# A gated linear recurrence and a PReLU feed-forward layer on one core: the written-out order of all steps is replaced by another order

## The chip, the cores and the metric

The kernel runs on one core of a Trainium2 chip. The metric is the device time of one execution in microseconds. An engine is named here as the profile names it: PE is TensorE (PEld its weight loads), DVE is VectorE, ACT is ScalarE, POOL is GpSimd, SP is SyncE, which in this kernel issues every transfer (731 of them).

## The reference, cut to what matters

```python
# attention block: batch 4, 8 heads, 768 tokens, head size 48
mag = np.sqrt(a_re * a_re + a_im * a_im)
scale = np.minimum(mag, 0.999) / (mag + 1e-06)
a_re_n, a_im_n = (a_re * scale, a_im * scale)      # one complex gate per token and channel
for t in range(S):
    new_re = ar * S_re - ai * S_im                 # ar, ai: the gates of token t
    new_im = ar * S_im + ai * S_re
    S_re, S_im = (new_re + k_t v_t^T, new_im)      # a 48x48 state per head
    y[:, :, t] = q_t @ S_re
# feed-forward block on x = y as 3072 tokens x 384
h = x @ w_in                                       # 384 -> 2048
g = np.maximum(h, 0.0) + alpha * np.minimum(h, 0.0)
out = g @ w_out                                    # 2048 -> 384
```

q, k, v and the gates are 32-bit floats; w_in and w_out arrive as 64-bit floats, and the kernel makes 32-bit ones of them. All products on PE are 32-bit.

## The kernel before, in words

The work is cut into 41 tasks. Each is a Python generator that emits one or a few instructions between two of its yields; such a piece is a *step*. There are 4292 steps. A task's own steps always come in the same sequence; how the steps of different tasks are mixed is written out by hand as a string of 4292 letters, `ORDER`, one letter for one step of the task with that letter:

```python
def run(self, order):
    for c in order:
        next(self.tasks[self.LETTERS.index(c)], None)
...
with tc.manual_schedule():
    ...
    plan.run(ORDER)
```

Every engine takes its instructions strictly in the sequence in which the steps emitted them, and so does SP with the transfers. A semaphore wait therefore holds up everything that stands behind it on its engine. `ORDER` thus sets the order on PE, DVE, ACT, POOL and SP together, and nothing else does. (The `yield DVE(...)`, `yield PE(...)` and so on only mark where a step ends; their numbers are not used.)

The tasks and their letters:

- **A to I: `gates`.** The gates of batch 0 in three pieces of 1, 2 and 3 chunks (A, B, C), then two pieces of 3 chunks for each other batch (D to I). A chunk is 128 tokens. A piece normalises the gates (ACT and DVE, lines 253 to 301), multiplies the magnitudes up into decays over 2, 4, 8, ... tokens (L318, stored as `decs`, L323), and multiplies the phases up along time: 7 products within blocks of 8 tokens, 7 over blocks of blocks (both `product`, L338 and L340, a multiplication and an addition), and a chain along the rest, `run` (the same two lines). After each of the two last stages `three` copies the result on ACT (L366, L368). Then come the normalisation of the offsets (L405 to L413), the last products (L426, L429, DVE), and the store of the phases, `phs` (L421, L431). In A, B and C the small products are DVE's, in D to I POOL's.
- **J: `loads`.** For each chunk: q and k into `KQ` (3 buffers, L579, L581), the phases into `PP` (1 buffer, L587), the decays into `T` (2 buffers, L594). `PP` reads what the gate piece stored in `phs`, `T` what it stored in `decs`.
- **K, L: `half_rows`, `loads_v`.** v in several arrangements, by way of a scratch in device memory (L560, L603 to L629).
- **M, N, O: `pieces`, `weights`.** The 16 pieces of the 64-bit weights (L491), and their conversion on ACT (L507, L509, L511), POOL (L515) and DVE (L517, L519).
- **P to Z and a to m: `unit`.** One for each of 24 chunks (4 batches of 6). A unit rotates q and k by the phases (L661, L663 on DVE, which read `PP`), and then goes through levels h = 1, 2, 4, 8, 16, 32: DVE scales `KQ` in place by the decays in `T` (L717), ACT makes copies (L740, L756), PE multiplies keys and queries (L678, `ps_lv`), ACT or DVE masks the result (L699, L702). Then PE transposes the keys (L785), ACT copies them over `T` (L787, L788), PE makes the chunk's state (L797, `ps_kv`) and the outputs (L817, L841, `ps_y`), DVE carries the state on (L826, L829), and ACT copies the output (L855), which SP stores (L860, `ysc`).
- **n: `loads_x`.** Reloads the outputs as `xT` (L873) in 14 token groups: 1, 1, ten times 2, 1, 1 chunks.
- **o: `all_mlp`.** The feed-forward layer. For each token group 16 features of 128 (three products each, L889, `ps_h`, 2 buffers), their PReLU (ACT L896, then DVE L898 into `g_sb`), and the output products (L908, `ps_o`), ACT copy (L918) and store (L921).

So the gates feed the units (by device memory), the units feed each other within a batch (the state) and the feed-forward layer (by device memory), and the feed-forward layer takes most of PE's time. Between two feed-forward products on PE stand the units' products, and all wait in one queue.

## Time and profile before

| | us |
|---|---|
| three runs | 851.10, 855.48, 854.49 |
| their median | 854.49 |
| the profiled execution | 854.34 |
| its span, first to last instruction | 852.6 |
| busy in the span: PE / PEld / DVE / ACT / POOL | 697.3 / 529.4 / 653.5 / 439.1 / 209.2 |

The profiled execution lies 0.15 us from the median, and 1.7 us of it lie outside the span. "Busy" counts the time in which at least one of the engine's instructions runs; an engine that only waits or issues is not busy. Each 32-bit product gives two records, so the 672 feature products are 1344 records in the profile.

The page's second part cuts the span into 40 slices of 21.3 us; a digit is the share of the slice in tenths. In the chain of waits, the profile follows the work that ended last back to what released it.

### The profile page before, as it was taken

What the parts mean: (1) busy time and instruction counts of PE and PEld (TensorE: products, weight loads), DVE (VectorE), ACT (ScalarE), POOL (GpSimd) and SP (SyncE); (2) the same over time, 40 slices, a digit from 0 to 9 for tenths busy, and PEclk for the clock granted to TensorE, in tenths of its full rate; (3) what the DMA queues carried; (4) which work ended last, traced back from release to release, by engine and by line L of the source; (5) the groups of instructions that cost most, each with busy time, mean ns of one, the idle gap of its engine ahead of it and who ended that gap; (6) DMA issues with size and microseconds to landing.
All of it is one profiled execution on the core that took longest, in us unless ns stands there. A gap on an engine that the chain in (4) does not pass through costs nothing.

```text
span 852.6 us, 26860 instructions
## 1 busy us (share of the span) xinstructions
PE 697.3 (82%) x11488; PEld 529.4 (62%) x11488; DVE 653.5 (77%) x1020; ACT 439.1 (52%) x937; POOL 209.2 (25%) x293
## 2 busy tenths in 40 slices
PE   0001314776998899889999999999999999999998
PEld 0001313565776677667777777777777777777776
DVE  5999999997996899599989997887776846633212
ACT  6767758766355754474576436554344334322221
POOL 6131232376403710260056144000052000000000
PEclk9999656798998999999999999999999999999999
DMA  8687876755768365756765766667454555412010
GB/s 238 155 272 188 263 200 189 216 128 138 203 174 199 102 182 163 209 133 156 231 156 145 212 162 177 157 182 185 113 130 104 148 143 117 102 46 65 11 39 9
DMA packets 194174, 130.91 MB, mean 154 GB/s; under 512 B 74120, under 2 KB 185864, under 8 KB 194056
## 3 DMA queue, kind: packets, MB, share of 16 engines
q1 hardware_dynamic: 194056, 129.20, 57.1%
q8 instruction: 90, 1.47, 0.7%
q14 instruction: 28, 0.23, 0.1%
HBM read 100.82 MB, written 35.71 MB: 160 GB/s over the span
## 4 chain that ended last, share of the span: by engine, by line
PE 63%; DVE 18%; POOL 6%; ACT 5%; DMA 4%; issue 3%; SPq 0%; DVEq 0%; ACTq 0%; POOLq 0%
PE ps_o L908 26%; PE ps_h L889 24%; PE ps_lv L678 4%; POOL gate L338 3%; PE ps_y L817 3%; DVE KQ L717 3%; PE ps_kv L797 2%; PE ps_y L841 2%; DVE gate L338 2%; DVE gate L426 2%; DMA T<-decs 2%; POOL run L340 2%; DVE gate L340 1%; PE ps_kt L785 1%; POOL gate L340 1%
## 5 line engine op out<-in xcount | busy, mean ns | idle before, releaser
L908 PE MATMUL ps_o<-w_out_sb,g_sb 128*128 128x384 f32 x768 | 297.9, 500 | 11.7 <-DVE g_sb L898 9.0
L889 PE MATMUL ps_h<-xT,w_in_sb 128*128 128x256 f32 (+1 forms) x1344 | 301.2, 357 | 0.0
L889 PEld LDWEIGHTS ps_h<-xT,w_in_sb 128*128 128x128 f32 x1344 | 235.1, 193 | 72.2 <-issue 3.3
L898 DVE SCALAR_TENSOR_TENSOR g_sb<-g_sb,al,ps_h 128x256 f32<-128x256 f32 (+1 forms) x224 | 97.3, 436 | 133.4 <-ACT g_sb L896 132.7
L896 ACT ACTIVATE g_sb<-ps_h 128x256 f32<-128x256 f32 (+1 forms) x224 | 79.1, 354 | 203.7 <-PE ps_h L889 202.7
L908 PEld LDWEIGHTS ps_o<-w_out_sb,g_sb 128*128 128x128 f32 x768 | 137.9, 192 | 63.0 <-DVE g_sb L898 12.0
L717 DVE TENSOR_TENSOR KQ<-KQ,T 96x1024 f32<-96x1024 f32 x120 | 146.6, 1225 | 33.9 <-PE ps_lv L678 22.9
L678 PE MATMUL ps_lv<-WQ 96*32 96x32 f32 x2304 | 34.3, 202 | 80.4 <-DVE WQ L661 51.8
L678 PEld LDWEIGHTS ps_lv<-WQ 96*32 96x32 f32 x2304 | 26.5, 115 | 98.1 <-DVE WQ L661 51.8
L338 POOL TENSOR_TENSOR gate<-gate 128x72 f32<-128x72 f32 x42 | 26.3, 626 | 148.3 <-ACT gate L368 145.5
L740 ACT COPY WQ<-KQ 96x1024 f32<-96x1024 f32 x48 | 50.0, 1041 | 15.4 <-DVE KQ L717 15.1
L515 POOL TENSOR_SCALAR top<-top 128x768 f32<-128x768 f32 x16 | 39.3, 2461 | 70.0 <-ACT top L507 59.7
L338 DVE TENSOR_TENSOR gate<-gate 128x576 f32<-128x576 f32 (+5 forms) x84 | 50.5, 601 | 1.7
L756 ACT COPY W<-KQ 96x512 f32<-96x512 f32 x48 | 30.8, 642 | 40.6 <-DVE KQ L717 33.1
L855 ACT COPY T<-ps_y 48x256 f32<-48x256 f32 x96 | 30.7, 366 | 36.8 <-PE ps_y L841 36.2
L817 PE MATMUL ps_y<-A,VL 64*48 64x64 f32 x2304 | 42.3, 227 | 3.7 <-issue 3.7
L785 PE MATMUL ps_kt<-ident,KQ 96*128 96x96 f32 x192 | 26.4, 264 | 22.2 <-DVE KQ L717 12.2
L426 DVE TENSOR_TENSOR gate<-gate 128x1152 f32<-128x1152 f32 (+2 forms) x36 | 44.2, 1250 | 0.1
L699 ACT ACTIVATE A<-ps_lv,columns 128x64 f32<-128x64 f32 x144 | 37.4, 337 | 13.0 <-PE ps_lv L678 12.9
L817 PEld LDWEIGHTS ps_y<-A,VL 64*48 64x48 f32 x2304 | 40.6, 128 | 4.4 <-issue 4.4
L785 PEld LDWEIGHTS ps_kt<-ident,KQ 96*128 96x128 f32 x192 | 22.1, 150 | 31.1 <-ACT T L788 10.9
L678 PE MATMUL ps_lv<-KQ,W 96*32 96x32 f32 x1536 | 24.2, 204 | 17.9 <-ACT W L756 17.9
(106 smaller groups left out, 926.9 us busy)
## 6 DMA issues: line engine op xcount, KB each, us to landing
T<-decs SPq DMA_DIRECT2D x48, 384.0 KB
PP<-phs SPq DMA_DIRECT2D x24, 387.0 KB
KQ<-in_q_dram SPq DMA_DIRECT2D x48, 192.0 KB
decs<-gate SPq DMA_DIRECT2D x7, 1152.0 KB
phs<-gate SPq DMA_DIRECT2D x14, 576.0 KB
KQ<-in_k_dram SPq DMA_DIRECT2D x40, 192.0 KB
vsc<-in_v_dram SPq DMA_DIRECT2D x48, 144.0 KB
VL<-vsc SPq DMA_DIRECT2D x24, 288.0 KB
```

Source lines behind the costliest of these rows:

```text
L338: on(4 * k).tensor_tensor(out=m, in0=w[:, 1::-1].unsqueeze(2).to_broadcast([P, 2, 2, k]), in1=pairs_of(u), op=ALU.mult)
L426: TT(out=m[:, a], in0=U5[:, 1 + a], in1=turned(off3, o)[:, a].unsqueeze(1).unsqueeze(3).to_broadcast([P, L // 2, nb, 2]), op=ALU.mult)
L515: nc.gpsimd.tensor_scalar(out=top, in0=top, scalar1=F64_SMALL, scalar2=None, op0=ALU.max)
L678: nc.tensor.matmul(t[64 * i + j:64 * i + j + HC // 2, p], lhsT=keys(n, g), rhs=queries(n, g), start=True, stop=True)
L717: nc.vector.tensor_tensor(out=x, in0=x if x0 is None else x0, in1=m, op=ALU.mult)
L740: nc.scalar.copy(z.rearrange("p i n t -> p i (n t)").rearrange("p i (m h) -> p m i h", h=h), bass.AP(tensor=KQ.tensor, offset=KQ.offset + ...
L785: nc.tensor.transpose(t[:, p], KQ[:, 1, 4 * i + p], ident[:D2, :D2])
L817: nc.tensor.matmul(o, lhsT=Vp[h][64 * i:64 * i + 64, s, e_ * D:(e_ + 1) * D], rhs=a, start=False, stop=False)
L889: nc.tensor.matmul(p, lhsT=w_in_sb[:, f // 2, kk, f % 2 * P:(f % 2 + 1) * P], rhs=x_of[m][:, kk], start=(kk == 0), stop=(kk == NK - 1))
L896: nc.scalar.activation(gt, p, AF.Relu, scale=-1.0)
L898: nc.vector.scalar_tensor_tensor(out=gt, in0=gt, scalar=al_1[:, f:f + 1], in1=p, op0=ALU.mult, op1=ALU.add)
L908: nc.tensor.matmul(sums[0], lhsT=gt[:, c * P:(c + 1) * P], rhs=w_out_sb[:, f], start=(f == 0), stop=(f == NF - 1))
```

## The change

The string `ORDER` is replaced by another string. It has the same 4292 letters, each as often as before. No other line differs, so that the instructions, their sizes and their data stay the same: 5888 matmuls, 707 two-input DVE operations, 935 ACT operations, 731 transfers in both programs. What differs is their sequence on PE, DVE, ACT, POOL and SP.

```diff
 ORDER = (
-    "AAAAAAAAAAAAAAAAAAAAABAAAAJMJJMABBBMMBANJMMAOAAAAAAAAAAAAAAAAAALLLNBLAAAAAAAAAAALNAAAAAAAKKKKKKKLLLA"
-    "OALLAMNNAAAAAAOAAAAAAAAABLBNAAAAAAALAANBBNOOBNBBBLBMBBBJOJNOBBBBBNBBJNNNBBNBBBBOBBBBBBBBBBBBBBBNOPBP"
-    "OBPPPPCCCBOKBBBBBBBBBBBBBPPOBBPKBCBBBMPCBPKKBCBJKKOPOPBBBBBBOMBKPNPMBBKNJBCKBBBBPPMBKKNKKBBNBPBBBBPP"
...
-    "oooooooooooooooooooooooooooooooooooooooooooooooooooooooooooooooooooooooooooooooooooooooooooo")
+    "AAAAAAAAAAAAAAAABJJJJBBAAAAAAAAMMMMMAMAAAAAAAAAAALLLBBNNBBLABLAAALABALAAAANBNABBBBANAABABBANABOOAMBB"
+    "OBBOAAAAAAKMAABBBABABABABABBAKKKKAALLKAABABABAABAABNAAAAABANBABALAAAABAABNBNOBBBBOOOOBONBMNBNNBBBBNNJ"
+    "OBOOOOOBBPBPCBNPCBBBBPCBBBBCCJJJOBBOBBKPPPPBCBBBBBMPNJJLNNBPNNBPBPBPBCNPBNCMBMCPPPPPJPCKKKKKKKKKKKKK"
...
+    "oooooooooooooooooooooooooooooooooooooooooooooooooooooooooooooooooooooooooooooooooooooooooooo")
```

More of the change, by code (lines that the diff above doesn't have):

```diff
@@ L30 @@
 ORDER = (
-    "AAAAAAAAAAAAAAAAAAAAABAAAAJMJJMABBBMMBANJMMAOAAAAAAAAAAAAAAAAAALLLNBLAAAAAAAAAAALNAAAAAAAKKKKKKKLLLA"
-    "OALLAMNNAAAAAAOAAAAAAAAABLBNAAAAAAALAANBBNOOBNBBBLBMBBBJOJNOBBBBBNBBJNNNBBNBBBBOBBBBBBBBBBBBBBBNOPBP"
-    "OBPPPPCCCBOKBBBBBBBBBBBBBPPOBBPKBCBBBMPCBPKKBCBJKKOPOPBBBBBBOMBKPNPMBBKNJBCKBBBBPPMBKKNKKBBNBPBBBBPP"
-    "BCCBPPOPCCCPPPNNPPCCCCPPCPPPPJLPPPPPJNCJPCNNNCCNCNCCQJQJPQJDDJJCPCJMNCNCPCPCPPCOCQQPDQDDJPPPPOCOOOCK"
-    "QCQCCCCCCQQCCCCCMOQCOJCJRCCRCOQOCOQQCQCOOOCCCCCCNNKKMMCCOCQCRCQCQCNNNKCLLLLLLQLCCCCCRQOCnCDCCCOCOCCC"
@@ L36 @@
-    "CQRMLLNDCJQCNRNRLLCQCCLLLRMCQCQDQRJJOCOCKQODCCCCRDNQQQQCCQQQQQQJODMQLNNDQODDODoQEKoooooooDOoRooNDJoo"
-    "oooooDRRQQRQLLoooDNoooLoRLLLLLDRLOQNQooQoQLooRRoRoDDoQDQDOOLDoooDDoRDELDLRRRRORRRRRJDooDDDDDDDRoooRN"
-    "NooDDRooooooEoRDRRRRRDNDoDoESDSDRDJOSREKOoooooLnoLLKoRSoooRRRRSSOLLKLSSSooESRLooooooLRoSOLLoLJELLSoo"
-    "NJSSSSoEoEESSDooDDooDDDDDDooooDDDDDDDKJREEoooDDDDooEDDDSDDoEooEoooSSSRSSSoLSooooJJSETSJSJJooKJSoEooo"
-    "DDDDDDooDESDSoooSSSDDDSSJEEoEETSSSSDESSSoSSSTEoooooooJJoKoEooDSDTooooEoSoTUKTLoTTTLoooooooooLTLoLoDK"
@@ L41 @@
-    "UooooooLDDTDJJooooJJnKDDDoEEooooDooTTETooDooooooLUoooooooooEoTToooUUDDLoooooooDTooToooooooDLDUUUoooo"
-    "ooUTUUooooooUoTTTTEoUUTTTTEooTTUToLLLLoooEEEToLooTTTTTTJJTTUoUUoTTUJoEooTETTTTTKEUUUUUFooooEUoooLLVo"
-    "oEoUooLLLELULLUVUoTUTVooUEEoooEULLLLLoooUUUJJJFEEUUUUUJJVVVUVVooooVVVJoUUUUUVVooFVooooUooVVoVFFVVoFV"
-    "LLVooEEEEEEEEEEEEEEEEoooEEEEoooooFFJoWVLLVWJFVoooJooooVooVVVVVWVoLVFooWoFoEEEoEVoVLWWLLLLLLELLVWVnVo"
-    "oJJEEEEEEJJFWooFEEEEEoWWoFFVFVJVFWVVoFoVooooooEWEWFVLVLVWWVWVVVVoooLKLooLLLoLLLJFFWWoXoWLJoEEoEEELEo"
@@ L46 @@
-    "ooooEooJooWWoEWEWWWEoooWEoEoooWWooFoWoWFoooooEXWWoooooLXoFoooooFFXoLXXWWWWXXWXFEXWXWWWXJJoooooJXXJXF"
-    "WXXFFFFoWWWWWoXoXooLoooWooooooXWLXXXXXooFoooXXFYoLLFFFFFFFoXXooXoXXoooLLLLLLLoooLLLYXXXJJXFJXFFFFFFF"
-    "FFFFooXYGooXXXGooYoooXXnFYJXXYYoFooYYXXXXYGooooYJJJoooooooooooJJYFFFFooJoooJooYYYYLGGoGZYYoooooooGGo"
-    "FFFFFFFooooFoYZoooFooFFoZooooZYYZYYZGYYZZoYYYoGZoYFFoYoooKKLLoYLLLLZLoLLLJLFFFFFLFLFFoZGGYoooooGZooG"
-    "GoGGYYoYYJJYoKKYGooYFFoFKKYoYLYLYLFLLLLYYLLLLFGaGZoYZFYYYFZZLZGKooooZooooLLoZKooFFFFFoooooZZZZaZZZZZ"
@@ L51 @@
-    "ooooZZoooooZooZoooJJFFGnooJoZZZZZFFFLooLFFZLZoZJLLLoGoaaGooooooooaZZaaGGJoGoooaooaLHaHaooGGoooGGGooa"
-    "ooooooooZZaZGGZZZoZaaaaaGGoooaHJoGoooooooaaaoaGGaaGaaaoooooGGaoLoaLoJoooooHHGboGGGGGGGaoHoaooLLobooL"
-    "LoooooJHHabJabHaaaaaabaJbJJaJaJaHaaabbbbbbbbHKoooooooHoooooooJGGGGoGGbbbHbGGooocGGGGbJHoooooooooooJG"
-    "GGKoooHbbccoooooooooobbccbGGGHcGbobbbGcGoooGGGGGGGGGHccooobbHGbGKLooooHHboobLLJLLLLLoLLLLLbLKnoobbcc"
-    "cHbbHJbcbcGHHHbHHbbcJoHHLLLLLLooLoLJLLHHHcooooocccHHoooooooooHGGGGbbbbbbbboGccccccGGocGGooocLoooooGo"
@@ L56 @@
-    "cLoccooooocLLGoGHGGooocJoooocGcccccccccccccJcccooKdooHooHoooJJJoHHHoJooHHHodHHHHoooooooooooHHHHdHHHH"
-    "HooHHdoodddJdJddddJJooeooooooooooooddoodddoooeoooddHHoooooooooHddeeeeoHHHHHLHHHHHHHLLLdddLLLLLdLLLLo"
-    "JLooeeddddodooHHddoJJeoooHdddHdddddneoooHHoIddeeeeeoodeJfLfIHdHHdHeddddooooeHooooLLLLooooooJJoooIIoo"
-    "oeooooIoooHoHHHooeeIoeeeHHHLfILoooHIooLooeIofHeJJoeooeooooIfffefoooeeLofoLoLoeLLLeeeeeeeeoJHfKHJJooo"
-    "oooofeoILLfooIeeHffffKLLLfoeLooeeeeeooooooofoooooooofoooLoofKffgooooffffffIffLILLLLJooIgHooooLfLfooo"
@@ L61 @@
-    "IooIKKIIIIoffffIfJnJfJHgfgJofIJJooooooofoooooogIfggfgoLoooffIIfLfffIogoKoggooooooooooooohhoogooooggg"
-    "ggoIhJhggoooooLoJoooooooooohhLJJooooghggggggghohogIILIIoogIoooggIogLLLLooooooIohhhhhooooLLLLgIoKKggg"
-    "ggggggJJJhhooohogggLIoooooooooIIIIIIKKoooogoghoIoooooioooLooooiJJIIoooooonIIIoohhhoiioooIIIIIoIhhhII"
-    "hhhLLLLLLLhhhiJiooILLLLLooIhJooohiohhooIIooooiiJhhhhhhIhIIiohooooiooLoLiLLLILiJIhhIhhhhhJiiIiiiiooII"
-    "IIIIIIIoooooooooooLiiiiIoIooooohhiiiiiiooojiooIIIIoooooIIoLjJJjjLooooLIooLiLoLLIjjjooooIooijjjjIIooo"
@@ L66 @@
-    "ooooiiiIiIIiiooiLooioooLLLiLLILoLLLIIjoiiijjoiiiioooIiojoooooooooojjjoooooooonojjjoooojjLjjjjjoooooI"
-    "jLjLLooooooojjoojjjjjjoooJJJJJoooJJoojJJjoooookokkJJoooooooooooojkjkLLjjjkjjojjkkoJkkoJJJkoookooooLL"
-    "LooooooooJlJlkkooooooooookokklooklokooooooloolkkkkokkklllLooookookLkoloLJkoooooooooLLkLLkLoLoooollkk"
-    "kkkkkkkkkkkkkoooooooooollllllooJoooooookkolooooollollmmnJJloooooooomooollooooooooollmllooooommlloooo"
-    "ooooooLLoLLoLoooLLLLLoLLLLooooomooooooommmmmoooollllllooolloooooolllllllllmmoooooooooLooLLLoooommooo"
@@ L71 @@
-    "oooooooooooooLoooooomoooooomooooLLLLLLLLmooonooooooooooommommooooooooooooooooooooooooommmmmmoooooooo"
-    "ooooooooommmooooooooooooooommmmmmmmmmmmomoommnoooooooooooooooooooooooooooooooooooooooooooooooooooooo"
+    "AAAAAAAAAAAAAAAABJJJJBBAAAAAAAAMMMMMAMAAAAAAAAAAALLLBBNNBBLABLAAALABALAAAANBNABBBBANAABABBANABOOAMBB"
+    "OBBOAAAAAAKMAABBBABABABABABBAKKKKAALLKAABABABAABAABNAAAAABANBABALAAABAABNBNOBBBBOOOOBONBMNBNNBBBBNNJ"
+    "OBOOOOOBBPBPCBNPCBBBBPCBBBBCCJJJOBBOBBKPPPPBCBBBBBMPNJJLNNBPNNBPBPBPBCNPBNCMBMCPPPPPJPCKKKKKKKKKKKKK"
@@ new lines @@
+    "BKBKPBBBMBCPBNOCNBOOBPCMNCLLCCBLPPPPPPPPPPPPPPPPCCMCBCCBKCCCPJOCOCDOJOCNNJCNNNNNCDCCKKKPCPCPPPPPPPPP"
+    "CCQCOKOOOCMQCCQLDDDQCCLLLLLLJLLLLLLCLCCCJDJJJJJJJCCNJQQCDNCQCQCDDQQCDCCNNQCDDQQDDQCOCODDCDCDCCCQDDOQ"
+    "CQOCQQQCDDDDKOCRQQCRQQQQQQCQQQRRRRQQQQQMnQCNDMCOCOOCDDDMCQCLQCLRCCCCRCRRLLLRCRRRoKJLQOOOOCoRoCoCRRCR"
+    "oQQLLLLLoooKLLQLoQQQoQCoCDCooRooQoRRDooCCCCRRRRRRRRRRoCRCoCoCoCDoRQCJJJEooRRODooooNNNNNoEDRooRoRoooo"
+    "RDnLLLLooOoOoOoRODLooRoLLLLLLRLLDNRNoLSoooooooooSoRRRRRooJJSooOoooooSoSSDSNDSSSESoooooooRoSNSSoooSDo"
@@ new lines @@
+    "ooSSSDJSJJEJJJJJJDoooooDoooEOSSSSooooSDoooSSSSSSooDDDDDDDooETTSSSEESooooSSSSSToSSEEESSooKSSSoSToJTTT"
+    "ToooToooSToooTooSLoooToULoDLLoLDTJDDDDDDJTDoToEDTDDoDLDLoDDDDDDooLLLLLoToTLTooooooooooToTTTUTTToTooT"
+    "ooTLJooDTTToooDUUTTTTTToULLLLULEEEEooEoTEoEDDDDDDDDDoDDEooooooUEToooUUUoooooonoUoEooJoUoooooUEUEDTDD"
+    "DoTTUUUELEJULoooLLKLLLLKoUoooooDDooDDDJoKDKKoKoooUUUUUUooooDDDTTTTTToUoooUDUUUooooUooDUEDUUUUEUEEEoo"
+    "EoEoooooooEoEEUooUooJooEoooUUUUoUUoFUUoooEEEoEoEooooooooooEEoEoEVFooFoJVVooJoFoJJnooooJJJJVJVFoLLooo"
@@ new lines @@
+    "oooooVVVFFLoLVoooooooooEEEEEEVoooVVVEEEEEEEEEEELEEEoEJJJooFoWWoEEoEEEVooooVVooVoooWJVVVVFLoooWooLooo"
+    "oWVVVVVVWVWWJVoooVFFVooooXVWLoLLLVLLoLooKVKoEEEEWEVVVVVVVVVVVKLLWEEVoKooLLLLLooLXFWLVLLVLVLVVWWWWWoE"
+    "EEEELooWooooEoEoEWEEEooJEWWWWWWWWEoooooooooJJEoEJEEEoooEWWWooooWoooWWWWWWWWWXLoooooWoFFFLXoLLXXXoXXo"
+    "GLLWWooJoJLLXooXoXWWWWWWooooFoFFXXXXXXFoLooooLooFoXoFoFFFFFFFJJooFooonXoXXXXXGLLLLooFFXooooooXXXXooo"
+    "XoXoFYFFFooooFoooFooXoFXXXXXXXXXFFXXXXXJJoYYJoooooLJLJFFFGoooFYLGFFFFFFFFooXoooYYYYYJYoYooXoooooooLo"
@@ new lines @@
+    "FFFFFoZZYYYYJooJYoYYZooooooYoooooZGoYYYYYYYYoYFLZZZZZZZFooooLoYYLFFLGFLLLLFLLooooYYoZZoYYYJYYYYJJLJJ"
+    "LLGoFZZZLLFLLFLLLLFLooooLFFFFFFFFFFFooZZYooFFFFYZoGGGGFoooFYYYYYYYYZZZoooFooLooooFFFFFFZJFFFZooZZZZZ"
+    "FZFoooooJZooZoZZnZZZZooZZZZZJZaZZLLFFJoLooooZZZJoooFoGaooGooaoaooooGGGLLLLLLLoLLLaaaaoooooooooaJaJaJ"
+    "ooooooaGaaaaaoooHoooHoaaooooooGGoooaaGaaaGGaaaGGGooGGGooboaaaKboooooJooooooaooooaHGbGaGJGbJoaaGaabbb"
+    "bJoJaaaaaabaaGLLbLLLoGoLGoLLLGaaHooHJooobboGoooooobboooGHobbbHobbooooJbooGHoJoboLHGJoooGbbbGbGbbbbJb"
@@ new lines @@
+    "ooocooooGoooJoonbooKoKGccoKKKKKooooooLbcccGcccooooHoooocooGoLLLbGJoJobbbobHbHGHHbbbLbHbGbbbbbLbbboGG"
+    "GGGHoHoHoLoooGGGGGoGcGLcoGoGooGGGoGoGoGcGcGcccccLJoJoLooLoooLooooLLLcccLLccLdocoJocGcoGcGccGoocodooc"
+    "oHHHddcHcccccccHdLcGGcGKoooLLHHGGHLoHLJLLHHoHooHooHooHdcGcdcdddcHcccooodoooGoooGGGGoGLLdLLLLLoGGGodd"
+    "dddoooododoooonooooGooGodGddddooGdoddoooooooGHGddHoodJodHHHoJoJJJHHHJJJooooodooooooddddddddddddddddo"
+    "HJeeooooJooooeoooooeoHooHHHHHHHdoLeeeooooooeeeeoefoofoooeeeoeoeooooJJooofLoooooLLooIeeofffeJeeooKooo"
@@ new lines @@
+    "oLLLLLLLLLHeeeeeeeeHHHHLooHoHoHoHeHoHeHooeeeeeeeeeeeeeeeJJIJJLLoHHeeHooHHIHfKHHfHHHHHoooHoJHoHooHffJ"
+    "ooHoofgIooogoooofffILoHHoofffHoofofHHogHooooLnooooLLLooLoJoLgLHKLffffffffggoLIILggggfoooofKooooKHooL"
+    "HooHgHooooHoHKKoKKHoofoIfKooofffoffffffffffLfJoJoofHfffHoooooHggggggoLLLLLooooIogoogIoooooHggIIIIooo"
+    "ooooLgoggLgLLLILoooogggggoooIgILoooogggggggggggggJJJoohJJhhoLLIIJoooJJoggLgoooJooohhILLLoIoInoooLoho"
+    "oiiJJhJohoLLJLLLhooooIIooooooooohhohhoIooooooihIhhhoIhhhoIIoIoIhIIIooiooooooooIIIihihhhhhhhooohLILIo"
@@ new lines @@
+    "oIooooIohooJJhJooohohoohhhhhIIIiIhIhhLhhhhLLoLooooiiiiooLoooLooooiiiooihohihhihooioioooooooJijJjiiJJ"
+    "JIIIIIIIIIIIIIIIIIIIIIIIIIIooiooooIojooiooioioioooooiooooIIijIIIoIIoojjjjjILoIiiIoILoLILoLoLLLiijiij"
+    "ioiLLLLLLLjjjLLLiLLoooIIIIIoooiooIIIIIiooooooooooooooijjjojojooLLoooooooojjjjijjjjIIiiiiooojoojooiii"
+    "jjjIooJjjjjjjjjjjjjnjoJJJjjjjooooooooooooookooookokokooLoooLJJJJJJJooooooLookkooookkokokookookooookk"
+    "kkkkkLLLooooooLLLLLLLoooookkkkoookkkkokooLookookkllokokkJkkkkkkkkkkkkkkololooooooooLLoooLooookLooLLL"
@@ L73 @@
+    "LllllllllLoLoooooooooJooooooooooooooooooooooonooooooooooooooooooJoooLLLollloooooooolllloooJooooooJJl"
+    "loooooJLlllllllllooooooooololoolllllllllllllllllooooooomooooLoooomoooooooooomooooommmmmmomooooomoooo"
+    "ooooLmmLmLLoooonooLomooooooooomLmmmLooooLLommmmmmmmoooooooomomomLLooooooooooomoooooooLomommmmmmmmmmm"
+    "mmmomooooooooooooooooooooooooooooooooooooooooooooooooooooooooooooooooonooooooooooooooooooooooooooooo"
     "oooooooooooooooooooooooooooooooooooooooooooooooooooooooooooooooooooooooooooooooooooooooooooo")
```

## The prediction

> **What bounds the kernel now.** I read the page's first two parts, then the busy times by stretch, then the waits of PE, then the chain of waits around the places where PE still stands.

> ```profile
> PE 697.3 (82%) x11488; PEld 529.4 (62%) x11488; DVE 653.5 (77%) x1020; ACT 439.1 (52%) x937; POOL 209.2 (25%) x293
> PE   0001314776998899889999999999999999999998
> DVE  5999999997996899599989997887776846633212
> PEclk9999656798998999999999999999999999999999
> ...
> 0.00:80.00 80.00, 3.94 (x192) 3.13 (x192) 67.56 (x163) 55.67 (x85) 26.69 (x39) 1.00 0.74 212
> 80.00:210.00 130.00, 65.41 (x1506) 53.41 (x1508) 122.48 (x192) 91.57 (x156) 55.83 (x51) 0.74 0.71 194
> 210.00:280.00 70.00, 66.94 (x1219) 51.68 (x1209) 60.35 (x92) 34.53 (x84) 19.06 (x27) 0.95 0.70 180
> 280.00:360.00 80.00, 74.10 (x1318) 55.27 (x1317) 66.38 (x92) 41.11 (x95) 23.52 (x37) 0.96 0.60 164
> 480.00:800.00 320.00, 320.00 (x4901) 240.07 (x4900) 214.66 (x306) 129.50 (x323) 38.05 (x78) 1.00 0.51 130
> ```

> The reader is to see a crossover. Until about 280 us DVE is busy nine tenths of the time and PE waits for it; from 480 to 800 us PE is busy without a hole. PE idles 76 us before 80, 65 us from 80 to 210, 3 and 6 us in the next two stretches, and not at all from 480 to 800. PE's work is the same in both programs, so the end can only move by PE time lost before about 480 us: by how much DVE work stands ahead of how much PE work while DVE is the bound.

> ```profile
> PE ps_kv L797 <- ACT T L788: 5.4, 1, 5.4
> ACT runs L366 <- POOL gate L338: 5.6, 1, 5.6
> ...
> 195.87 5.53 POOL gate L338
> ...
> 255.32 7.41 DMA T<-decs
> ```

> The first two lines are waits between 186 and 210 us, the others pieces of the chain (start, length). At 199 us ACT stands behind gate piece D's chain on POOL, and unit S's copies, and so PE, stand behind ACT. At 255 us unit V has to wait for its decays: `T` is free only when unit T has been stored.

> **The change, part by part.** No instruction is added or removed, so the work terms are zero. What moves is the order, and I count it as follows. Each instruction keeps the time for which it held its engine in the trace of before (DVE's sum to 653.5 us); PE's are taken at their mean spacing after 300 us (0.41 us for a product of L889, 0.66 us for one of L908; 687.4 us in all). Both programs' queues are then walked in the order of their steps, and at the first feature product of a token group I read how much DVE work and PE work stand ahead of it. Measured time less DVE work is DVE's idle time so far; measured time less PE work is the PE time lost so far. For the changed program I keep DVE's idle time.

> | token group | measured us | DVE ahead | PE ahead | DVE idle | lost before | lost after |
> |---|---|---|---|---|---|---|
> | 1 | 194.1 | 178.2 to 175.0 | 50.9 to 52.0 | 15.9 | 143.2 | 138.9 |
> | 2 | 231.7 | 210.4 to 214.2 | 88.2 to 94.5 | 21.3 | 143.5 | 141.0 |
> | 3 | 288.6 | 260.6 to 246.5 | 134.9 to 130.2 | 28.0 | 153.7 | 144.3 |
> | 4 | 355.1 | 316.3 to 303.6 | 190.3 to 185.4 | 38.8 | 164.8 | 157.0 |
> | 5 | 413.1 | 365.8 to 358.4 | 244.0 to 243.8 | 47.3 | 169.1 | 161.9 |
> | 6 | 468.8 | 421.8 to 405.9 | 297.8 to 293.9 | 47.0 | 171.0 | 159.0 |

> Group 4, for instance: 303.6 + 38.8 - 185.4 = 157.0. The new order puts 7 to 16 us less DVE work ahead of nearly the same PE work from group 3 on. Lost time doesn't come back, so group 6 has to be read as the 161.9 of group 5: 171.0 - 161.9 = **9.1 us less**. It could be 12.0 if group 5's idle shrinks too. Behind group 6 only 3 us more are lost (174.2 at group 8), and I leave them.

> *Waits that get more cover.* Between unit T's last product and unit V's first use of its decays lie 27.9 us of DVE work instead of 10.5; the wait took 14.0 us. Beside the `run` chain of piece D lie 14.2 instead of 6.3 us until ACT asks for it, beside E's 14.9 instead of 8.7; the chains took 13.6 and 15.6. The holes in PE behind these were 5.4 us (ps_kv at 205.8) and 2.6 us (ps_lv at 264.8), so the worth lies between 0 and 8 us. I take **2 us**, near the low end, because some of it is already in the table's smaller loss.

> *Waits that get less cover.* From the last DVE operation of a gate piece until its first unit's L661 the phases must be stored and loaded again.

> ```profile
> 32.45 0.56 DVE L429 TENSOR_TENSOR gate<-gate 128x384 f32<-128x384 f32 x1
> ...
> 33.04 0.36 SPq L431 DMA_DIRECT2D phs<-gate  x1
> ...
> 36.05 0.33 SPq L587 DMA_DIRECT2D PP<-phs  x1
> ...
> 50.53 1.22 DVE L661 TENSOR_TENSOR WQ<-KQ,PP 96x1024 f32<-96x1024 f32 x1
> ```

> For piece A the operation ended at 33.0, the load was issued at 36.05, and its last packet landed at 41.2: 8.2 us. The DVE work between the two shrinks from 17.0 to 7.4 us, so DVE stands 0.8 us. For C it shrinks from 29.5 to 9.2, where 12.4 us passed (143.0 to 155.4): 3.2 us. D has 11.6 for 10.0 us: nothing. G has 8.8 for 13.7: 4.9 us, but there PE has work queued. The `run` chain of F has 4.2 for 11.4 us: up to 7.2 us on ACT, which holds the PReLU and so PE's two `ps_h` buffers. The sum lies between 0 (each transfer and chain as fast as the fastest seen, 7 us for B's phases and 4.7 us for I's chain) and 0.8 + 3.2 + 4.9 + 7.2 = 16 us. I take **3 us**: A's and C's for the most part, since the other two fall where PE is backed up. The end of the queue needs no term: before the last group's first product PE has 30.3 instead of 17.1 us of other work, and the reload took 13.3.

> Sum against the profiled execution: 854.3 - 9.1 - 2 + 3 = 846.2, so **846 us**; the median of the runs shown is 0.2 us above that execution.

> [...] The change is described as made for random cases of late transfers and late instruction packets. In the trace PE waits with nothing but "issue" to show in two groups only, one of them just behind an instruction packet at 343.1 us:

> ```profile
> PE ps_y L817 <- issue: 3.7, 2, 1.9
> PE ps_o L908 <- issue: 2.5, 1, 2.5
> ```

> So late packets were worth at most 6.2 us of PE in that run, and the sum has no term for them. [...] On POOL the row is the 5.53 us above, for a product of 12 elements per partition that takes 0.23 us elsewhere in the same chain, with two-input DVE operations back to back beside it. [...]

> **The rivals.**

> *The gain comes with its covers.* If V's and D's holes close wholly (8 us instead of 2) and the shrunk covers cost little (0 to 3), the sum is 854.3 - 9.1 - 8 + 0 to 3 = 837 to 840. For it: both holes stand in the chain of waits. Against it: a chain that is freed usually meets the next one.

> *Nothing that shows.* DVE's idle time is not a constant. The loads that a unit needs leave on SP in one queue, behind stores that wait for ACT. If they leave as late as before, DVE has less to do and waits for them: the 9 us turn into DVE idle time, and with 3 us for the covers and 2 us back the time is about 854. Against it: in the trace DVE waited for a transfer once, for 2.3 us at 262.8.

> *Slower: the way of the phases.* One mechanism, at P, S and V, the first units of A, C and D: DVE stands until the phases are back, and while DVE is the bound each us is a us at the end. Covers are 7.4, 9.2 and 11.6 us for ways of 8.2, 12.4 and 10.0 us. To pass 0.5% above, the standing must exceed 8.1 + 4.3 = 12.4 us beyond the sum's. If SP issues `PP` behind a store or a weight piece that waits, as at C (5 us of its 12.4), and each of the three ways is 7 us longer, DVE stands 21 us and the time is 854.3 - 8.1 + 21 = 867. For it: the new order puts gate inputs, V parts and weight pieces between these. Against it: SP's longest waits for a weight slot, for V's buffer and for decays in the trace are 7.8, 5.4 and 8.1 us, each once.

> That the change doesn't do what it says can be left out: the order differs from the first DVE rows on.

> **How the numbers follow.** Half a per cent (4.3 us) is about what a measurement of this kernel can tell from no change. My forecast (840 to 850) has 0.47, the larger gain 0.15, no visible change (850.2 to 858.8) 0.15, slower 0.23. So faster 0.62, same 0.15, slower 0.23. Low end: 854.3 - 12.0 - 8 = 834. High end: every shrunk cover costs its most and no longer cover pays, 854.3 - 9.1 + 16 = 861; 863 takes in the slower case with 5.7 us of standing on each of the three ways (854.3 - 8.1 + 17).

> **What would show it right or wrong.** Right: the first feature product of group 3 near 274.5 (246.5 + 28.0), that of group 6 near 456 (293.9 + 161.9); PE's idle time near 147 us instead of 155; no piece of 7 us for `T<-decs` near 260, no wait of 5.6 us of ACT on POOL near 200. Wrong: DVE idle well above 28 us at group 3; waits of DVE L661 on `PP`; holes in PE after 480 us.

## The result, and the profile after

The changed kernel takes **846.26 us** (median of 20 runs, 840.63 to 857.29); the kernel before, run beside it, 851.12 us (846.51 to 855.48). The ratio is 0.9933, with a 95% interval of 0.9911 to 0.9955: 0.7% or some 6 us faster. The profiled execution took 847.24 us with a span of 845.2 us. The one shown of before (854.34 us) lay 3.2 us above the median of its 20 runs, so the two profiles differ by 7.1 us and the medians by 4.9 us. The comparison of traces below has to carry this difference.

The page's first two parts and the busy times by stretch, of the kernel after (columns: length of the stretch, busy time and instructions of PE, PEld, DVE, ACT and POOL, granted clock, DMA share, GB/s):

```profile
PE 699.6 (83%) x11488; PEld 529.6 (63%) x11488; DVE 653.3 (77%) x1020; ACT 443.3 (52%) x937; POOL 196.3 (23%) x293
PE   0002316688899999999999999999999999999998
DVE  5999998689998999979998997687877656345212
...
80.00:210.00 130.00, 76.41 (x1641) 60.36 (x1645) 116.14 (x190) 81.58 (x148) 37.09 (x31) 0.91 0.74 203
210.00:280.00 70.00, 67.69 (x1063) 52.71 (x1053) 64.83 (x93) 41.93 (x95) 37.54 (x49) 1.00 0.76 191
280.00:360.00 80.00, 80.00 (x1537) 60.21 (x1536) 76.66 (x105) 46.87 (x104) 20.47 (x35) 1.00 0.69 179
480.00:800.00 320.00, 312.60 (x4782) 234.36 (x4781) 212.50 (x302) 129.40 (x323) 37.11 (x80) 1.00 0.51 127
```

PE does 11 us more between 80 and 210 us and stands no time at all from 280 to 360. Its idle time over the span is 845.2 - 699.6 = 145.6 us, where it was 852.6 - 697.3 = 155.3. But between 480 and 800 us, where the old order had no hole, 7.4 us of PE are now idle. The experiments go after that stretch too.

The waits of DVE between 195 and 362 us, before and then after (engine, line and tile, releaser: us in total, times, longest):

```profile
DVE g_sb L898 <- ACT g_sb L896: 8.4, 8, 2.3
DVE KQ L717 <- ACT T L855: 4.1, 1, 4.1
DVE KQ L717 <- PE ps_lv L678: 3.9, 4, 2.6
DVE St L829 <- PE ps_kv L797: 3.6, 1, 3.6
DVE KQ L717 <- ACT WQ L740: 3.5, 3, 2.6
DVE KQ L717 <- DMA T<-decs: 2.3, 1, 2.3
```

```profile
DVE g_sb L898 <- ACT g_sb L896: 4.9, 11, 1.0
DVE KQ L717 <- PE ps_lv L678: 1.3, 3, 0.7
DVE KQ L717 <- ACT WQ L740: 0.9, 3, 0.4
```

25.8 us of waits became 7.1. Unit S's wait for its state (`ps_kv`), unit V's for its decays (`T<-decs`) and the one for ACT's copy L855, in unit Y's time, are gone.

The same method as in the prediction's table (PE time lost = time less the PE work done so far) gives, for before and after and for three kernels of the experiments:

| PE work done, us | before | after | new to 200, then old | old to 200, then new | old to 60, then new |
|---|---|---|---|---|---|
| 60 | 150.0 | 146.3 | 146.4 | 148.9 | 147.5 |
| 100 | 144.8 | 142.4 | 142.5 | 144.2 | 147.8 |
| 200 | 165.7 | 146.8 | 148.3 | 162.1 | 152.1 |
| 220 | 168.2 | 150.1 | 158.8 | 164.2 | 155.7 |
| 400 | 173.8 | 159.3 | 165.9 | 174.2 | 169.5 |
| 600 | 179.5 | 171.3 | 171.9 | 186.2 | 182.2 |

At 200 us of PE work (346.8 us of the run after, 365.7 before) the new order is 18.9 us ahead; at 600 us it is 8.2 us ahead. So more was won than forecast, and over half was given back in a stretch to which the prediction gave no term. The table has one execution of each kernel. Six executions that have the new order up to 200 us of PE work have lost 141 to 151 us there, four that have the old one 159 to 166; the means lie 16 us apart. The experiments go after the lead and the give-back.

### The profile page after: what moved, and what is told of

Same layout as the page of the kernel before. It is cut to its first block, busy times and chain, and to the rows that moved or that the text cites. A ratio compares the mean times of both kernels' runs of the same rounds, so it can differ in the third digit from the quotient of the medians.

```text
span 845.2 us, 26866 instructions
## 1 busy us (share of the span) xinstructions
PE 699.6 (83%) x11488; PEld 529.6 (63%) x11488; DVE 653.3 (77%) x1020; ACT 443.3 (52%) x937; POOL 196.3 (23%) x293
## 4 chain that ended last, share of the span: by engine, by line
PE 63%; DVE 17%; DMA 6%; issue 6%; ACT 5%; SPq 2%; POOL 0%; DVEq 0%; ACTq 0%; POOLq 0%
PE ps_o L908 25%; PE ps_h L889 25%; PE ps_lv L678 4%; DVE KQ L717 4%; PE ps_y L817 3%; PE ps_kv L797 2%; PE ps_y L841 2%; DVE gate L338 2%; DMA PP<-phs 2%; DMA phs<-gate 1%; DMA g_sb<-in_w_in_dram 1%; PE ps_kt L785 1%; DVE gate L426 1%; SPq L626 1%; DVE gate L340 1%
## 5 line engine op out<-in xcount | busy, mean ns | idle before, releaser
L889 PE MATMUL ps_h<-xT,w_in_sb 128*128 128x256 f32 (+1 forms) x1344 | 302.0, 356 | 2.9 <-DVE g_sb L898 1.6
L908 PE MATMUL ps_o<-w_out_sb,g_sb 128*128 128x384 f32 x768 | 295.2, 499 | 5.1 <-DVE g_sb L898 4.9
L889 PEld LDWEIGHTS ps_h<-xT,w_in_sb 128*128 128x128 f32 x1344 | 234.3, 193 | 74.1 <-issue 3.6
L908 PEld LDWEIGHTS ps_o<-w_out_sb,g_sb 128*128 128x128 f32 x768 | 138.0, 192 | 56.7 <-DVE g_sb L898 6.9
L717 DVE TENSOR_TENSOR KQ<-KQ,T 96x1024 f32<-96x1024 f32 x120 | 148.5, 1239 | 32.1 <-PE ps_lv L678 23.2
L678 PE MATMUL ps_lv<-WQ 96*32 96x32 f32 x2304 | 34.7, 204 | 79.0 <-DVE WQ L661 55.9
L678 PEld LDWEIGHTS ps_lv<-WQ 96*32 96x32 f32 x2304 | 26.6, 116 | 99.7 <-DVE WQ L661 56.1
L338 POOL TENSOR_TENSOR gate<-gate 128x72 f32<-128x72 f32 x42 | 29.6, 704 | 125.6 <-ACT gate L368 122.8
L855 ACT COPY T<-ps_y 48x256 f32<-48x256 f32 x96 | 30.8, 364 | 51.8 <-PE ps_y L841 51.2
L338 DVE TENSOR_TENSOR gate<-gate 128x576 f32<-128x576 f32 (+5 forms) x84 | 50.0, 595 | 1.1
L515 POOL TENSOR_SCALAR top<-top 128x768 f32<-128x768 f32 x16 | 41.5, 2602 | 32.1 <-ACT top L507 32.1
L678 PE MATMUL ps_lv<-KQ,W 96*32 96x32 f32 x1536 | 25.2, 205 | 27.5 <-ACT W L756 23.2
L817 PE MATMUL ps_y<-A,VL 64*48 64x64 f32 x2304 | 42.4, 223 | 4.1 <-DMA VL<-vsc 2.5
L699 ACT ACTIVATE A<-ps_lv,columns 128x64 f32<-128x64 f32 x144 | 36.2, 336 | 17.2 <-PE ps_lv L678 17.1
L817 PEld LDWEIGHTS ps_y<-A,VL 64*48 64x48 f32 x2304 | 39.8, 124 | 5.5 <-DMA VL<-vsc 2.7
L678 PEld LDWEIGHTS ps_lv<-KQ,W 96*32 96x32 f32 x1536 | 20.3, 115 | 29.6 <-ACT W L756 24.7
L785 PE MATMUL ps_kt<-ident,KQ 96*128 96x96 f32 x192 | 26.0, 260 | 15.4 <-DVE KQ L717 12.9
```

The source lines that it names most:

```text
L338: on(4 * k).tensor_tensor(out=m, in0=w[:, 1::-1].unsqueeze(2).to_broadcast([P, 2, 2, k]), in1=pairs_of(u), op=ALU.mult)
L515: nc.gpsimd.tensor_scalar(out=top, in0=top, scalar1=F64_SMALL, scalar2=None, op0=ALU.max)
L678: nc.tensor.matmul(t[64 * i + j:64 * i + j + HC // 2, p], lhsT=keys(n, g), rhs=queries(n, g), start=True, stop=True)
L699: nc.scalar.activation(a[:, :, cols], t[:, :, at:at + name], AF.Copy, scale=s)
L717: nc.vector.tensor_tensor(out=x, in0=x if x0 is None else x0, in1=m, op=ALU.mult)
L817: nc.tensor.matmul(o, lhsT=Vp[h][64 * i:64 * i + 64, s, e_ * D:(e_ + 1) * D], rhs=a, start=False, stop=False)
```

## Experiments

**1 and 2: half of each order.** Steps taken from one order up to a letter, then the steps not yet taken, in the sequence of the other. The place of the change is called the seam.

```diff
-ORDER = OLD
+ORDER = NEW[:1789] + the remaining steps as in OLD      # new to 200 us of PE work
+ORDER = OLD[:1816] + the remaining steps as in NEW      # old to 200 us of PE work
```

> The new order up to 200 us of PE work (letter 1789), then the rest of the steps in the old order. In the profiles the new order leads by 18.9 us there (346.8 against 365.7 us) and ends with a lead of 7.1. If the lead of DVE work over PE work sets the lost time (theory 1), the old rest, which has 366.1 us of DVE work ahead of group 5 for 244.0 of PE, loses 366.1 + 33 - 244.0 = 155 us by then and no more later, against 171 before: about 16 us under the old kernel, 835. If the covers of single waits made the gain (theory 2), they all lie in the first part, and the time is 833 to 836 too. If the 11 us that the new order gives back are chance (late instruction packets in that one profile) and not its own, the time is the new kernel's, 843 to 848, with the same losses now and then.

> The old order up to 200 us of PE work (letter 1816), then the rest in the new order. The PE time lost by then is the old 165 us. Theory 1: the new rest has less DVE work ahead (355.9 against 366.1 at group 5), so the 6 us that the old order loses between there and group 6 are saved; if the new rest also loses its own 11 us afterwards, 851 - 6 + 10 = 855; if those were chance, 845 to 847. Theory 2 (covers of V, D and E, all in the first part): no gain, 851 to 860.

New, then old: 845.59 us, 0.9923 of before (0.9895 to 0.9952). Old, then new: 861.63 us, 1.0131 (1.0081 to 1.0181). The first is as fast as the whole new order, and not 10 us faster; the time alone would speak for chance. The table above shows that it isn't. The kernel has the whole lead at 200 us of PE work (148.3 us lost), as the new order has. That also speaks against the granted clock as the cause of the lead. Between 80 and 210 us it was 0.74 before and 0.91 after, but 0.76 in this kernel:

```profile
80.00:210.00 130.00, 75.96 (x1624) 60.40 (x1627) 116.47 (x190) 81.96 (x148) 37.02 (x30) 0.76 0.74 203
```

Whether the clock has a small part in the medians is open: in each of three sets of runs of the kernel before, the executions with a granted clock over 0.975 have a median 1.2 to 4.4 us below that of the others, and 14 of the 20 runs of the kernel after had such a clock.

The kernel with the new order first then loses 10.5 us within the next 20 us of PE work. From 220 to 600 us it loses 13.1 us, much as the old order does (11.3). Its waits of PE between 346 and 376 us and its busy times there:

```profile
PE ps_lv L678 <- ACT W L756: 4.5, 2, 3.0
PE ps_lv L678 <- ACT WQ L740: 1.6, 1, 1.6
...
346.00:376.00 30.00, 22.54 (x414) 16.33 (x413) 23.97 (x28) 19.39 (x37) 22.61 (x35) 0.89 0.45 106
```

PE stands 7.5 us there. A likely cause is what the new order has put off. Between the first products of groups 4 and 5 DVE is busy for 64.4 us in this kernel, 49.9 in the old order, 56.6 in the new one. At the seam the new order is 15 steps of gate piece F, 8 of unit Y and 4 of gate piece G behind the old one, whose remainder wants them at once. That this work alone costs the 10.5 us is not shown: DVE, too, stands 6.0 of these 30 us.

Old, then new shows the other half. The new order's late part loses 22.0 us from 220 to 600 us of PE work, and 21.2 us in the whole new order, where the old one loses 11.3. The kernel of experiment 11, also new from there on, loses 26.5. It happens in three executions with different pasts, so the give-back belongs to the order, not to chance.

**3 and 4: the feed-forward steps moved as a block.** Steps of o (and n) between letters 1250 and 2450 put behind 40 other letters, in the new order; steps of o ahead of up to 40 other letters, in the old one.

> The new order, with only the letters of the feed-forward layer and of its reloads between letters 1250 and 2450 set back behind 40 letters of other tasks. The steps of gates, units and loads keep their sequence. DVE work less PE work ahead of groups 3, 4 and 5 grows from 115.8, 114.1 and 112.1 to 126.3, 122.4 and 122.9 us, about the old order's 122.8, 125.2 and 122.1. Theory 1: about 10 us slower than the new order, 854 to 858. Theory 2: the covers of V's decays and of the chains of D and E are what they were, so the time stays at 845 to 849.

> The old order, with only the feed-forward letters between letters 1250 and 2450 moved ahead of up to 40 letters of other tasks, not ahead of the reload of their tokens. DVE work less PE work falls at group 4 by 2.4, at group 5 by 9.1 and at group 6 by 5.1 us; groups 3, 7 and later stay. Theory 1: the 6 us that are lost between groups 4 and 6 are mostly saved, 845 to 847. Theory 2: no cover of the old order's waits is changed for the better, 850 to 853, or slower where a product now stands in PE's queue before its tokens have come.

939.85 us, 1.1037 of before (1.0987 to 1.1087), and 901.17 us, 1.0594 (1.0549 to 1.0638). Both expectations missed by far. DVE's main wait between 255 and 480 us, in the new order and in the first of the two:

```profile
DVE g_sb L898 <- ACT g_sb L896: 7.3, 14, 1.0
```

```profile
DVE g_sb L898 <- ACT g_sb L896: 43.4, 27, 4.8
DVE KQ L717 <- PE ps_lv L678: 13.2, 10, 3.0
DVE KQ L717 <- ACT WQ L740: 5.9, 7, 3.0
```

A feature passes PE, ACT, DVE and PE again, and a level of a unit DVE, PE or ACT, and DVE again. My reading is that once the two kinds of step no longer alternate as they were placed, each round trip holds up what stands behind it in every queue (in the traces of before and after the tasks' 1009 DVE rows, 267 POOL rows and 731 transfers stand in the order of their steps); no run takes the round trips apart. How much DVE work stands ahead of how much PE work, the prediction's measure, says nothing of this.

**5 to 8: the instruction stream of PE.** In the traces of before, after and the two halves, many of PE's late stops come just behind a 16 KiB packet of the instruction queue. The page of before has 90 of these:

```profile
q8 instruction: 90, 1.47, 0.7%
```

```profile
650.59 0.29 PE L808 MATMUL ps_y<-ident,nothing 64*48 64x256 bf16 x4
650.70 1.71 PE L817 MATMUL ps_y<-A,VL 64*48 64x64 f32 x96
652.34 0.46 PE L678 MATMUL ps_lv<-WQ 96*32 96x32 f32 x32
652.61 0.42 PE L678 MATMUL ps_lv<-KQ,W 96*32 96x32 f32 x24
655.22 0.27 PE L678 MATMUL ps_lv<-KQ,W 96*32 96x32 f32 x8 [2.18 <-issue]
```

(L808 is bf16; all other products on PE are 32-bit.) These small matmuls go by at one in 8 to 17 ns (32 records in 0.27 us, 96 in 1.64). The block from 651.0 us was worked through in 1.8 us; the next packet began at 653.0 and took 0.96 us; PE went on at 655.2, in the middle of a run of matmuls that all have their data. To test that it is the block and not the step, I moved the block borders and nothing else: small matmuls into the first `ps_lv` tile, which the real ones then overwrite, run while PE has nothing to do before 51 us.

```diff
+    idle = []
...
             t = shared[0][:, at]
+            if u == 0 and ("met", 0, 0) not in done and not idle:
+                idle.append(u)
+                for _ in range(64):       # 128 instructions; 116, 128 and 8 in the others
+                    nc.tensor.matmul(t[0:32, 0], lhsT=nothing[0:64, 0:32],
+                                     rhs=ident.bitcast(BF16)[0:64, 0:32], start=True, stop=True)
```

> The old order, with 64 small matmuls that nothing reads put ahead of TensorE's first real one: 128 more instructions (a weight load and a matmul each) that run while TensorE has nothing to do, before 51 us. No step is moved; only the places where TensorE's instruction stream goes from one block of 256 instructions (16 KiB, one packet of queue 8) to the next lie 128 instructions further along in the kernel's own work. In the traces so far TensorE's unexplained stops stand exactly at these places, and behind blocks that TensorE had worked through in about 2 us. Theory 'instruction packets': the old order has few such blocks as it stands (the shortfall of its blocks below 3.6 us sums to 3.0 us after 200 us) and about 15 with the shift (20.6 us), so the time rises by 8 to 18 us, to 860 to 869 us for 851.5 before, and new stops of 1 to 2.5 us appear late in the run, where the old order had none. Rival 'order of the waits': these stops belong to certain steps and not to the blocks; then the time stays within 1.5 us and the stops stay at the same matmuls.

> The new order with the same 128 instructions ahead. Theory 'instruction packets': the shortfall of the blocks goes from 12.9 to 24.2 us; the stops at 369, 538, 625, 655 and 756 us go, others come in greater number: 5 to 11 us slower than the new order alone, 851 to 857 us. Rival: within 1.5 us of 846, stops at the same matmuls.

> The new order with 116 such matmuls, 232 instructions, ahead: the blocks begin 24 instructions earlier than without. Theory 'instruction packets': this is the shift with the smallest shortfall for the new order, 7.2 us for 12.9; the time falls by 2 to 6 us, to 840 to 844 us. Rival: within 1.5 us of 846.

> The old order with 128 small matmuls, 256 instructions, ahead of TensorE's first real one, twice as many as in the kernel that took 25 us longer. They fill one whole block, so that the later blocks begin again at the same matmuls as in the old order. Theory 'instruction packets': back within 3 us of the kernel before (850 us), with two stops at block crossings after 200 us as there. Rival 'the extra matmuls themselves cost the time': 50 us longer than before, or at the least the same 25 us.

| order | instructions ahead | us | ratio to before (95%) | stops at borders after 200 us, sum |
|---|---|---|---|---|
| old | 0 | 851.1 | 1 | 2, 4.8 us |
| old | 128 | 873.41 | 1.0293 (1.0249 to 1.0338) | 17, 30.6 us |
| old | 256 | 851.39 | 0.9999 (0.9974 to 1.0024) | 5, 7.6 us |
| new | 0 | 846.26 | 0.9933 (0.9911 to 0.9955) | 6, 10.2 us |
| new | 128 | 875.51 | 1.0307 (1.0267 to 1.0346) | 17, 33.4 us |
| new | 232 | 843.66 | 0.9935 (0.9904 to 0.9966) | 6, 9.7 us |

Half a block costs 25 us and a whole block nothing, though it has twice as many added matmuls. The stops are the block's. (The sums take in stops down to 0.3 us.) The waits of PE on nothing but issue from 210 to 800 us, in the old order with 128 and with 256 instructions ahead; the added lines make L817, L678, L841 and L908 into L824, L685, L848 and L915:

```profile
PE ps_y L824 <- issue: 10.7, 8, 2.2
PE ps_lv L685 <- issue: 8.8, 6, 4.3
PE ps_y L848 <- issue: 3.2, 3, 1.2
PE ps_o L915 <- issue: 2.7, 1, 2.7
```

```profile
PE ps_y L824 <- issue: 4.3, 3, 1.7
PE ps_o L915 <- issue: 2.0, 1, 2.0
PE ps_lv L685 <- issue: 0.3, 1, 0.3
```

In the new order the loss agrees with the stops within one pair of traces: 33.4 - 10.2 = 23.2 us more of stops, 872.53 - 847.24 = 25.3 us more of time. In the old order the medians are 25.0 us apart (873.41 against 848.43 beside it) and the stops 30.6 - 4.8 = 25.8, but these stops come from an execution that was only 13.1 us longer than the one shown of before (867.40). It was some 6 us ahead at 200 us of PE work, and PE's other waits between 210 and 800 us sum to 2.9 us instead of 6.6, so part of its stops fall where PE stood before for another reason. Over ten of the traces, after 200 us, the stop goes with the time that a block takes:

| block worked through in | blocks | with a stop over 0.5 us | mean stop |
|---|---|---|---|
| under 2 us | 40 | 85% | 1.5 us |
| 2 to 2.5 us | 23 | 74% | 1.3 us |
| 3 to 4 us | 31 | 32% | 0.6 us |
| 5 to 7 us | 170 | 2% | 0.05 us |
| over 7 us | 439 | 0 | 0.01 us |

Between these bands a stop followed 4 of 14 blocks of 2.5 to 3 us and 8 of 78 of 4 to 5 us, counted over all fourteen traces. The old order had no block under 3 us after 200 us, the new one has nine, and the old one shifted by 128 has fifteen. The 232 show the limit of this: they were chosen to leave the fewest short blocks, and did (four), but three stops of 1.8 to 2.4 us came behind blocks of 3.3 to 5.9 us whose next packet started only 3.5 to 5.7 us after the block began. The old order's own two stops are of this kind: blocks of 3.6 and 5.2 us, packets 3.9 and 4.9 us after they began. No gain shows. What holds a packet back was not tried.

**9 and 12: new early, old late, with the seam elsewhere.** The letters up to 3300 as in the new order, the rest as in the old; then the same with 16 instructions ahead.

```diff
-ORDER = OLD
+ORDER = NEW[:3300] + the remaining steps as in OLD
```

> The new order up to its letter 3300, and the remaining steps in the old order: the seam lies where the two orders have the same work of VectorE behind them (about 555 us of it at 460 us of TensorE work). From here on the old order lost 3.8 us against its matmuls and the new 8.3 us, most of it in three stops at instruction blocks (625, 655 and 756 us). Theory 'instruction packets, set by the order of TensorE's stream': about 842 us, 4 us under the new order. Rival 'the lead is used up in any order': 845 to 847 us.

> The hybrid of the new order up to letter 3300 and the old one behind it, with 8 small matmuls (16 instructions) ahead. By the passage times of its blocks this is the best of all shifts for it, with a sum of likely stops of 8.9 us for 10.8. Theory 'instruction packets': 1 to 4 us faster than the hybrid alone (840.7 us, 0.990 of before), 0.985 to 0.989 of before. Rival: no difference that shows, 0.990.

840.66 us, 0.9899 (0.9861 to 0.9937), and 850.20 us, 0.9989 (0.9954 to 1.0023). By the interval the first is not distinct from the new order's 0.9933, and the second contradicts what was expected: its stops sum to 9.0 us, not less than the 7.1 us of the first. Its interval lies wholly above the first's, about 0.9% slower, more than the 1.9 us of stops explain. In the traces it is 2.9 us behind at 200 us of PE work and 6.8 us at 400, where the steps are the same and the seam is yet to come; why is open. In the trace of the first, the seam costs 4.2 us more than the new order loses at that place, and the old remainder saves 4.4. Its profiled run is 5 us ahead because it was so at 200 us already, where its order is the new one. No hybrid is shown to beat the new order.

**10: the gates' place.** The new order with the steps of F to I where the old order has them, measured by the PE work ahead of them.

```diff
-ORDER = NEW
+ORDER = NEW, with each step of F, G, H, I at the PE work that OLD has ahead of it
```

> The new order with the steps of the gate groups F, G, H and I put back to where the old order has them, by the TensorE work ahead of them; every other step stays where the new order has it. VectorE's work ahead of feed-forward groups 3, 4, 5 and 6 goes from 246.0, 299.5, 355.9, 405.1 to 248.6, 306.9, 363.0, 412.4 us; TensorE's stream is the same. Theory 'VectorE's work ahead' (the first term of the prediction): group 4 starts 7 us later (338 for 331 us), groups 5 and 6 as well; at the end 3 to 7 us slower than the new order, 849 to 853 us. Rival 'covered waits alone' (the whole early gain is the stops that the interleaving of units and feed-forward steps hides, and the gates' place does not matter): group 4 within 2 us, the time within 2 us of 846.

920.73 us, 1.0815 (1.0764 to 1.0866). It doesn't separate the two theories. Group 4 starts at 352.7 us instead of 331.4: DVE has been busy 7.7 us longer by then (306.0 for 298.3 us), as expected, but 13.6 us is new DVE idle time. Its wait of DVE for the PReLU between 255 and 480 us (7.3 us in the new order):

```profile
DVE g_sb L898 <- ACT g_sb L896: 24.5, 22, 3.1
```

As in 3 and 4, steps put in at places that fit another order cost more than the work that they move.

**11: the start.**

```diff
-ORDER = OLD
+ORDER = OLD[:923] + the remaining steps as in NEW       # old to 60 us of PE work
```

> The old order for its first 923 letters (60 us of TensorE's work, to about 208 us of the run), then the remaining steps in the new order. Tells whether the new order's start, to which the prediction gave nothing by itself, has a part in the 19 us that it is ahead by 200 us of TensorE work. Theory 'the middle alone' (gates later, waits of units S, V, W and Y covered): within 2 us of the new order, 845 to 849 us. Rival 'the start matters': the 3.7 us by which the new order is ahead at 60 us of TensorE work, or more, are missing: 850 us and above.

853.22 us, 1.0020 (0.9994 to 1.0045). The time is the rival's: no gain is left. But the table puts little of that into the start itself. At 60 us of PE work, the seam, 1.2 us is missing, at 100 us 5.4, at 200 us 5.3, and the late part takes 5.6 us more. Most of what is missing early is lost just behind the seam, so this kernel can't tell the start's worth from the seam's cost. The other traces can bound the start: at 60 us of PE work, eight executions that begin with the new order have lost 140.2 to 146.4 us (mean 143.7), six that begin with the old one 146.7 to 150.0 (mean 148.3). So the start is worth some 4.6 us at that point, where one execution differs from the next by up to 6 us.

## Why the prediction was right, and where its terms were not

The time came out as predicted, and the direction with it. Of the signs that it named, these came: group 3's first feature product at 274.1 us (274.5 predicted), PE idle 145.6 us (147), no wait of DVE for `T<-decs` left between 195 and 362 us, none of ACT for POOL near 200 us. Group 6 came at 447.6 us, earlier than the 456 predicted. The sum hit, however, because two misses cancelled: the lead was under-sized, and the give-back had no term. That is luck.

**The table of token groups: too small from group 4 on.** PE time lost after, predicted and then measured: group 1 138.9 and 143.0, group 2 141.0 and 141.5, group 3 144.3 and 143.9, group 4 157.0 and 146.0, group 5 161.9 and 150.6, group 6 161.9 and 153.7. At group 4 the order had won 18.8 us, not 7.8. When group 4 began, DVE had been busy for 298.3 us, for 315.8 before. That is 17.5 us of work put off, where the prediction has 12.7 (303.6 of 316.3). Less the 4.9 us of PE work that has moved behind group 4 as well, it makes 12.6 of the 18.8 us. The other 6.2 us is DVE's idle time, 33.1 us instead of 39.3. At group 3 the sum was right and its parts were not: DVE 243.0 us busy and 31.1 idle, for 246.5 and 28.0. One pair of executions overstates it a little. Over six with the new order up to here and four with the old one the lead at group 4 is 17 us, of which 3.5 is idle time, so most of the lead is work put off.

**More cover: -2 us, mis-sized.** The change in DVE's idle time is a net. Up to group 1 DVE idles 9.3 us more in the new order (25.5 us for 16.2); from there to group 4 it idles 15.5 us less (7.6 for 23.1), and there stood the waits for S's state, V's decays and ACT's copy that have all vanished. The trace of before shows 5.4 us of PE at `ps_kv` as one event; in five more kernels that begin with the old order it is 5.9, 4.7, 4.2, 2.8 and 1.8 us, and in the new order 1.1. The hole thus belongs to the old order and only its size varies. The prediction feared that a freed chain meets the next one; here it met none until 360 us.

**Less cover: +3 us, not where it was put.** The first units of A, C and D did not wait for their phases, so the slower rival falls. F's `run` chain took 5.8 us where 11.4 had been feared, and ACT did not wait for it. What DVE idled more before group 1 was for PReLUs (5.9 us for 2.6) and for POOL (L517, 4.6 us), which no term had. The phases came late elsewhere, at the first two units of the last batch:

```profile
DVE WQ L661 <- DMA PP<-phs: 5.2, 3, 2.6
593.64 1.13 PE L889 MATMUL ps_h<-xT,w_in_sb 128*128 128x256 f32 x4 [0.84 <-DVE g_sb L898]
```

The first line sums DVE's three waits after 500 us. Of these, DVE stands 2.6 us until 588.1 and 2.2 us until 598.6, comes late to the PReLUs behind, and PE stands 0.8 us for them at 593.6 and again at 603.3. So the sign "waits of DVE L661 on `PP`" came in a small way, for some 1.6 us of PE.

**"Behind group 6 I leave them": the step that failed.** The prediction carried the lead of group 6 to the end. In fact the new order loses 24.5 us from 200 to 600 us of PE work, the old one 13.8. Of the 10.7 us between them, 5.9 are stops at block borders (8.1 against 2.1), 3.3 are four short waits of PE that the old order hasn't (421, 484, 594 and 603 us; the last two are those behind the phases), and 1.5 are spread. The prediction's "wrong if: holes in PE after 480 us" came true, without spoiling the sum.

**Late instruction packets: no term, and a loss.** The prediction puts them at 6.2 us at most in the run of before, with no term in the sum. It saw one stop of before behind a packet; the other, 1.9 us that end at 382.0, stands behind one as well. The new order loses 5 us more at the block borders than the old one did (10.2 for 4.8 us). Whether a border costs anything goes with the time that the block takes: none of the 439 blocks over 7 us ended in a stop over 0.5 us, and four fifths of the 63 under 2.5 us did.

**The stretched operation on POOL.** In the trace after, the largest operation of D's `run` chain takes 1.29 us (5.53 before); other executions of the old order have operations of 2.5 to 4.0 us at this place. F's chain was not stretched (5.8 us, its largest operation 1.95 us). That points at what stands beside D's chain in the old order; no run shows what of it stretches the chain.

The rival "the gain comes with its covers" (837 to 840) has the lead of group 6 right, 9.1 + 8 = 17.1 us for 17.3 measured, and would have had the time, had the give-back not come. Its split is not what the traces show: the work put off is the larger part. Two sums of the prediction's rivals are loose, without bearing on the forecast: 854.3 + 3 - 2 is 855.3 and not 854, and with 7 us more on each way the covers given leave 7.8 + 10.2 + 5.4 = 23.4 us of standing, not 21.

## What to carry to other kernels

In these kernels PE stood where its stream goes from one packet of 256 instructions to the next: 85% of the 40 blocks that it passed in under 2 us ended in a stop over 0.5 us, and none of the 439 that took over 7 us. To look for the same elsewhere, number the instructions, look for blocks that are passed in a short time (under 3 us here), and test with a shift of half a block in PE's idle time, since here that moved the time by 3% with no step moved. An order that puts work off may only have borrowed the time (10.5 us came back at one seam): look at where the work must be done, and whether the engine has slack there. And where four in-order queues pass data in circles, moving one kind of step by tens of places cost 6% and 10% here (901.17 and 939.85 us), so the sum of work ahead is a measure for orders that are close to each other, not for arbitrary ones.

## What the runs showed that I had not expected

PE went on 2.2 to 2.9 us after its instruction packet began, although the packet itself took 0.9 to 1.4 us (four stops of the new order: 369.0, 625.0, 655.2 and 756.4 us). Nor did I expect that such a packet starts only 0.6 to 2 us after PE has entered the block ahead of it (the same four), and in three cases of the shift by 232 only 3.5 to 5.7 us after. On average a block had to last some 3.4 us to hide the next one, an estimate from the traces: block and stop together averaged 3.3 to 3.6 us where the block took under 2.5 us. A third of the blocks of 3 to 4 us ended in a stop all the same.
